# Attention with an ELU feed-forward on one core: another order of the first stage, and six weight tiles kept in PSUM

## The chip, the core and the metric

The kernel runs on one core of a Trainium2 chip. A core has TensorE (PE in the profile, with PEld for its weight loads), VectorE (DVE), ScalarE (ACT), GpSimd (POOL) and SyncE (SP), which here only issues transfers. Each engine works through its own instructions strictly in order and waits for the others by semaphores. PE writes to PSUM, which has eight banks; the other tiles lie in SBUF. The metric is the time of one execution on the device in microseconds; 608.86 before the change (median of three runs, 608.73 to 609.06).

## The reference

```python
scores_l = scale * q @ k^T, where |i - j| < 16, else -1e9          # local window, head size 64
scores_s = scale * q @ max over 32 keys of k + log(32)             # 24 block summaries
a = exp(scores - max);  a = a / (sum(a) + 1e-9)
x = a @ concat(v, mean over 32 of v)                               # 4 batches x 768 tokens x 512
h = x @ w_in                                                       # 512 -> 2048
g = where(h > 0, h, exp(min(h, 0)) - 1)
out = g @ w_out                                                    # 2048 -> 512
```

All is float32. The kernel multiplies in the format fp32r and splits each factor into a high half (rounded to fp32r) and a low half (what is left), and adds three products: high x high, low x high, high x low.

## The kernel before

The 3072 tokens go through the feed-forward in 6 chunks of 512, each in 16 steps f of 128 hidden columns. Step (c, f) makes `h` (12 products of 128x512, layer 1), takes `e = exp(h)` on ACT, forms the activation on DVE, splits it into `gh` and `gl`, and adds 12 products into four PSUM banks `o0` to `o3` (layer 2). The attention for the tokens of the next chunk runs between the steps, in groups of two pairs of heads: scores (`gsc`), maximum and mask on DVE (`glow`), exponentials on ACT (`ge`), reciprocal (`gz`), normalisation (`gn`), transposes (on PE, `gtr` with a copy `gpc`, or on DVE, `gb`), product with the values (`gval`), and the split of the result (`gxh`, `gxl`).

The first chunk is different. Its own attention has to run first (the words without a g: `sl`, `ss`, `low`, `exp`, `z`, `norm`, `tr`, `ptc`, `val`, `xh`, `xl`; `sums`, `spr` and `mv` make and spread the means of the values), and during its 16 steps the 32 weight tiles are loaded and split. Tile j (w1_f or w2_f) is loaded as 64-bit words (`w.j`), its lower bits are scaled on POOL or ACT (`X`, `Y`), its exponent is moved by ACT into a PSUM tile `sh` in bank a0 or a1 by j mod 2 (`M`), DVE joins the parts in two instructions into an SBUF tile `cv` with two buffers (`S`), the high half is cast (`H`, a second number 0 for ACT, 1 for POOL), and the low half is subtracted (`L`, 0 for POOL, 1 for DVE). The banks a0 and a1 also hold the scores and transposes of the attention groups. `first`, `L1h`, `L1l`, `L2a`, `L2b` and `L2c` are PE's products of chunk 0; `E`, `gap` and `larger` make the activation from h, `G` and `gl` split it.

The order of all this, on all five engines, is a list of words by hand, `FIRST`; each word stands for one such step (`name.arguments`), and each engine gets its instructions in the list's order. Short products into unused banks (`idle`, `warm`) fill PE's gaps before the first layer-1 product. Behind the list follows a loop over the remaining 80 steps, in which only PE and SP are in program order; a scheduler places the instructions of the others, and it may place the loop's first instructions between the last ones of the list.

Line numbers below are those of the kernel before: 152 and 155 the two joining instructions, 161 and 164 high and low half of a weight, 184 exponentials, 188 to 193 sum, reciprocal and normalisation, 202 transposes, 426 the first value products, 470 the first layer-1 products, 690 and 730 layers 1 and 2 of chunk 0, 679 and 740 the same in the loop, 695 the exponential of h, 699 and 710 the loop's minimum and sum.

Of the kernel before, what the change touches and what calls it, by code (L numbers as in the profile page):

```python
# [40 lines left out]
FIRST = """  # L41
    kq.2 mh.0 kq.3 sl.0 ve.3 ve.0 w.0 ve.1 mh.1 ss.0 idle.1.188 low.0.0 max.1 low.0.1 sl.1 idle.1.260 ss.1 ve.2
    max.2 exp.0.0 vo low.1.1 exp.0.1 exp.1.1 w.1 z.0 norm.0.1.0 norm.0.0.0 low.1.0 exp.1.0 w.5 max.3 sl.2 w.2 ss.2
    low.2.0 exp.2.0 z.1 norm.1.0.0 low.2.1 exp.2.1 sl.3 idle.1.232 ss.3 low.3.0 low.3.1 w.3 exp.3.1 z.2 tr.0.1.0
    tr.0.0.1 w.4 warm.2.288 sums.0 sums.1 warm.1.88 X.0 norm.1.1.0 ptc.0.0.0 norm.2.1.0 norm.2.0.0 exp.3.0 ptc.0.1.0
    w.7 sums.2 spr.3.0 spr.0.0 mv.0.0.0 tr.1.0.3 ptc.1.0.1 zh.3.1 sk.0 spr.2.0 spr.1.1 norm.3.1.0 mv.0.1.0 mv.0.2.0
    tr.2.1.1 w.9 warm.1.164 ptc.2.1.0 w.6 tr.2.0.0 ptc.2.0.1 mv.1.1.0 M.0 tr.1.1.2 ptc.1.1.1 mv.1.2.1 M.1 X.1 zh.3.0
    val.0.0 mv.0.3.0 mv.1.3.0 tr.3.1.0 ptc.3.1.1 norm.3.0.1 tr.3.0.0 mv.1.0.2 val.0.1 ptc.3.0.1 val.1.0 xh.0.0 S.0
    S.1 val.2.1 xl.0 val.1.1 xh.1.0 xl.1 H.0.1 val.2.0 xh.2.0 L.0.0 val.3.0 val.3.1 w.18 xh.3.0 xl.2 xl.3 first.0
    first.1 M.2 H.1.0 q.0 first.2 Y.5 first.3 X.2 S.2 X.3 L.1.0 X.4 L1h.1 M.3 S.3 E.0 gap.0 sk.2 vm.0 H.3.1 H.2.0  # L50
    sv.0 M.4 L1l.1 larger.0 G.0.0 L1h.2 L.3.0 L1l.2 sk.3 gl.0.0 L2a.0 w.10 w.16 M.5 E.1 L.2.1 Y.6 X.7 S.4 H.4.0
    L.4.0 S.5 M.6 ts.1 H.5.0 stt.1 L2c.0 L2b.0 G.1.0 L2a.1 L2c.1 L.5.0 M.7 gl.1.0 w.8 E.2 S.6 H.6.1 L.6.0 gap.2 S.7
    H.7.0 vs.0 larger.2 G.2.0 ks.3 sk.1 X.10 gsc.0 glow.0.0 L1h.3 glow.0.1 ge.0.0 w.13 L.7.1 X.9 ks.1 gl.2.0 gz.0.0
    X.8 M.8 gn.0.0.0 M.9 w.17 L1l.3 E.3 S.8 H.8.1 L.8.0 S.9 H.9.1 gap.3 larger.3 w.11 X.11 M.10 ge.0.1 S.10 L2b.1
    L2a.2 L2c.2 L1h.4 L1l.4 gz.0.1 gn.0.1.1 L2b.2 q.1 M.11 E.4 gtr.0.0 G.3.1 gl.3.0 gap.4 L.9.1 S.11 H.10.0
    gpc.0.0.1 L1h.5 w.12 X.13 M.12 w.19 X.12 w.20 gtr.0.1 larger.4 G.4.1 L.10.1 S.12 gpc.0.1.1 H.11.0 L.11.0 M.13
    S.13 vm.1 L1l.5 w.15 X.20 E.5 H.12.0 gap.5 H.13.0 L2a.3 X.17 larger.5 ks.2 L2c.3 vl gval.0 w.14 gsc.1 gl.4.1
    glow.1.0 sv.1 G.5.0 gxh.0 X.16 X.14 M.14 L1h.6 L1l.6 gxl.0 L1h.7 ge.1.0 E.6 glow.1.1 M.15 L.12.0 S.14 H.14.0
    L.13.0 X.15 L1l.7 X.18 ks.0 S.15 X.19 gz.1.0 gap.6 gn.1.0.0 L2b.3 gl.5.0 L2a.4 sv.2 L2b.4 L2c.4 pm.2 K.3 L.14.1
    w.25 M.16 S.16 gtr.1.0 larger.6 ge.1.1 gz.1.1 L2a.5 H.15.0 L.15.0 vs.2 M.17 S.17 H.16.0 gn.1.1.0 gpc.1.0.1 M.18  # L60
    w.23 pm.3 E.7 gap.7 L2b.5 L2c.5 X.25 G.6.1 H.17.0 gl.6.0 gtr.1.1 gpc.1.1.1 M.19 L.16.1 S.18 H.18.0 L1h.8 L1l.8
    larger.7 gval.1 G.7.0 sv.3 vs.3 L.17.0 S.19 E.8 gl.7.0 gxh.1 w.22 vs.1 gxl.1 q.2 K.2 gsc.2 H.19.0 gap.8 glow.2.0
    L2a.6 L2b.6 L2c.6 L.19.0 w.30 larger.8 ge.2.0 L1h.9 L1l.9 L.18.0 X.22 w.24 glow.2.1 M.20 gz.2.0 ge.2.1 mmul S.20
    gn.2.0.1 M.22 w.21 gz.2.1 mact X.23 E.9 L2a.7 L2b.7 L2c.7 X.24 L1h.10 L1l.10 gn.2.1.1 w.28 gb.2.0.4 M.21 X.30
    gap.9 X.21 larger.9 G.8.1 gl.8.0 H.20.0 L.20.0 S.21 gb.2.4.8 w.26 H.21.1 M.23 L.21.0 S.23 E.10 G.9.1 gl.9.0
    L1h.11 w.31 L1l.11 S.22 H.23.1 E.11 gb.2.8.12 gap.10 H.22.0 gap.11 larger.10 larger.11 M.25 q.3 w.29 L2a.8 L2b.8
    M.24 L2c.8 G.10.0 L.22.0 S.24 L2a.9 L2b.9 L2c.9 L.23.0 S.25 X.26 gl.10.1 L1h.12 mm G.11.1 X.29 L1l.12 E.12
    gap.12 H.25.0 w.27 X.27 gsc.3 gb.2.12.16 gval.2 K.4 gxh.2 gl.11.1 H.24.1 L2a.10 L2b.10 X.28 L2c.10 L.24.0
    glow.3.1 M.27 glow.3.0 L.25.0 gxl.2 S.27 H.27.1 L.27.0 M.26 S.26 H.26.1 ge.3.0 L1h.13 L1l.13 larger.12 M.29
    ge.3.1 gz.3.0 gn.3.0.0 S.29 E.13 gap.13 L1h.14 M.28 G.12.1 gz.3.1 L2a.11 gn.3.1.1 gl.12.0 L1l.14 E.14 L2b.11  # L70
    gap.14 X.31 L2c.11 L2a.12 L2b.12 L.26.1 gb.3.0.4 L2c.12 M.31 larger.13 H.29.0 L.29.0 larger.14 L1h.15 L1l.15
    S.28 H.28.1 gb.3.4.8 S.31 L.28.0 M.30 S.30 G.13.0 gl.13.0 gb.3.8.12 H.30.1 L.30.0 G.14.0 gl.14.0 E.15 gap.15
    H.31.0 L2a.13 L2b.13 L.31.0 gb.3.12.16 larger.15 L2c.13 L2a.14 q.4 gsc.4 glow.4.0 gval.3 gxh.3 gxl.3 L2b.14
    glow.4.1 ge.4.1 gz.4.1 ge.4.0 gn.4.1.1 G.15.1 gl.15.0 L2c.14 gz.4.0 gn.4.0.1
"""
# [846 lines left out]
```

## Time and profile before

| | |
|---|---|
| median of three runs | 608.86 us (608.73 to 609.06) |
| the profiled execution, and its span | 608.52 us, 606.8 us |
| PE busy in the span | 598.2 us, 99% |
| DVE, ACT, POOL busy | 64%, 43%, 40% |
| granted TensorE clock | 0.999 |
| moved from and to HBM | 50.8 MB read, 6.3 MB written |

The profile is of one execution; all times in it count from the span's start, and some 1.7 us of the execution's time lie outside the span. Products on PE are pipelined: one of 128x512 is shown with about 0.39 us, but the next starts 0.227 us later. So PE's pace is read from the starts, and its waits from the idle time in brackets.

### The profile page before, as it was taken

Reading aid. Unit: us, or ns where it says so; the run is one execution under the profiler, and the core shown is the slowest. Engines: PE = TensorE matmul, PEld = TensorE weight load, DVE = VectorE, ACT = ScalarE, POOL = GpSimd, SP = SyncE. Lnnn points to the kernel's source line nnn. Section 1 sums busy time; section 2 is a strip of 40 time slices with the busy share of each in tenths; the row PEclk is TensorE's granted clock in tenths of the full one; section 3 lists DMA queues with packets and bytes.
Section 4 is the critical chain, followed back from the end, with each engine's and each line's share of the span. In section 5 each row is a group of like instructions: output and inputs, shape, how many; then the busy total and the mean of one; then the engine's idle time right before and its main releaser. Section 6 shows DMA issues by size and latency. Waiting matters only on the chain.

```text
span 606.8 us, 11202 instructions
## 1 busy us (share of the span) xinstructions
PE 598.2 (99%) x4105; PEld 489.4 (81%) x4105; DVE 391.3 (64%) x1099; ACT 261.9 (43%) x754; POOL 245.7 (40%) x285
## 2 busy tenths in 40 slices
PE   9999999999999999999999999999999999999997
PEld 7787888878888888888888888888888888888885
DVE  7999989977667875656767676566575563222122
ACT  6987875654243343442433424425424332322222
POOL 5898998742333332332323323323133232222221
PEclk9999999999999999999999999999999999999999
DMA  9999783141005225220063132303111000100001
GB/s 313 376 362 310 219 292 85 32 136 47 23 27 146 78 72 177 71 66 0 28 174 109 53 94 80 102 2 107 60 38 42 2 1 0 70 0 1 0 1 69
DMA packets 63694, 58.62 MB, mean 97 GB/s; under 512 B 22664, under 2 KB 55176, under 8 KB 63640
## 3 DMA queue, kind: packets, MB, share of 16 engines
q1 hardware_dynamic: 60328, 52.02, 28.7%
q10 hardware_dynamic: 3312, 5.90, 2.6%
q8 instruction: 32, 0.52, 0.3%
q14 instruction: 22, 0.18, 0.1%
HBM read 50.82 MB, written 6.29 MB: 94 GB/s over the span
## 4 chain that ended last, share of the span: by engine, by line
PE 88%; DVE 5%; DMA 2%; issue 2%; ACT 1%; SPq 0%; DVEq 0%; ACTq 0%
PE h L679 36%; PE o L740 36%; PE o_ps L643 4%; PE o L730 4%; PE h L690 3%; PE s L586 3%; DMA vxh<-in_v_dram 2%; DVE sh L152 2%; DVE pt L624 1%; DMA kn<-in_kT_dram 1%; DVE cv L155 1%; PE t_ps L202 1%; PE o_ps L426 1%; DVE e L707 1%; PE h L470 0%
## 5 line engine op out<-in xcount | busy, mean ns | idle before, releaser
L720 POOL TENSOR_TENSOR gl<-e,gh 128x512 fp32r<-128x512 f32 x93 | 120.2, 1293 | 262.6 <-ACT gh L715 151.5
L679 PE MATMUL h<-xh,w 128*128 128x512 f32 x640 | 212.4, 393 | 0.0
L740 PE MATMUL o<-w,gh 128*128 128x512 f32 x648 | 163.0, 389 | 0.0
L740 PEld LDWEIGHTS o<-w,gh 128*128 128x128 f32 x648 | 121.7, 188 | 25.2
L679 PEld LDWEIGHTS h<-xh,w 128*128 128x128 f32 x640 | 120.2, 188 | 25.9
L695 ACT ACTIVATE e<-h 128x512 f32<-128x512 f32 x96 | 57.1, 595 | 182.9 <-PE h L679 169.4
L624 DVE STREAM_TRANSPOSE pt<-sm 32x256 f32<-32x256 f32 x288 | 125.6, 436 | 6.4 <-POOL sm L193 1.4
L699 DVE TENSOR_SCALAR e<-e 128x512 f32<-128x512 f32 x81 | 41.9, 517 | 133.7 <-ACT e L695 133.3
L679 PE MATMUL h<-xl,w 128*128 128x512 f32 x320 | 124.7, 390 | 0.0
L715 ACT CAST gh<-e 128x512 fp32r<-128x512 f32 x88 | 54.5, 621 | 103.9 <-DVE e L710 102.9
L740 PE MATMUL o<-w,gl 128*128 128x512 f32 x324 | 89.6, 389 | 0.0
L184 ACT ACTIVATE sm<-sm,mx 128x120 f32<-128x120 f32 x160 | 61.2, 385 | 24.0 <-DVE mx L176 24.0
L740 PEld LDWEIGHTS o<-w,gl 128*128 128x128 f32 x324 | 60.8, 188 | 12.6
L679 PEld LDWEIGHTS h<-xl,w 128*128 128x128 f32 x320 | 60.1, 188 | 11.9
L193 POOL TENSOR_TENSOR sm<-sm,z 128x480 f32<-128x480 f32 x34 | 35.9, 1075 | 64.0 <-DVE z L196 62.6
L710 DVE SCALAR_TENSOR_TENSOR e<-h,e 128x512 f32<-128x512 f32 x81 | 56.0, 692 | 2.8
L176 DVE CUSTOM_DVE_ANT_0 sm<-s,mask 128x120 f32<-128x120 f32 x160 | 34.2, 278 | 22.1 <-PE s L586 22.1
L690 PE MATMUL h<-xh,w 128*128 128x512 f32 x120 | 39.4, 395 | 0.0
L164 POOL TENSOR_TENSOR w<-cv,w 128x512 fp32r<-128x512 f32 x25 | 33.0, 1327 | 4.5 <-ACT w L161 3.5
L657 DVE TENSOR_TENSOR xl<-o_ps,xh 128x256 fp32r<-128x256 f32 x40 | 15.1, 419 | 26.3 <-ACT xh L650 26.3
L730 PE MATMUL o<-w,gh 128*128 128x512 f32 x120 | 31.8, 395 | 0.0
L184 ACT ACTIVATION_READ_ACCUMULATOR sm<-sm,mx 128x1 f32 x160 | 30.2, 189 | 0.0
(121 smaller groups left out, 555.5 us busy)
## 6 DMA issues: line engine op xcount, KB each, us to landing
...
```

The source lines that it names most:

```text
L184: nc.scalar.activation(out=sm[:, t, :], in_=sm[:, t, :], func=AF.Exp, bias=mx[:, t, :], scale=-1.0, accum_out=z[:, t, :])
L193: engine.tensor_tensor(out=sm, in0=sm, in1=z.broadcast_to([P, UW, KC]), op=ALU.mult)
L624: nc.vector.transpose(out=dst[k, :, q], in_=src[q, :, k])
L679: nc.tensor.matmul(h_ps, w[:, a, cols], bb[:, cc, :], start=(k == 0), stop=(k == 3 * NCC - 1))
L690: nc.tensor.matmul(h_ps, w[:, lo, cc * P:(cc + 1) * P], bb[:, cc, :], start=(lo, cc, i) == (0, 0, 0), stop=(lo, cc) == (1, NCC - 1))
L695: nc.scalar.activation(out=e, in_=h_ps, func=AF.Exp)
L699: nc.vector.tensor_scalar(out=e, in0=e, scalar1=1.0, scalar2=-1.0, op0=ALU.min, op1=ALU.add)
L710: top = nc.vector.scalar_tensor_tensor(out=e, in0=h_ps, scalar=0.0, in1=e, op0=ALU.max, op1=ALU.add)
L715: copy(out=gh, in_=e)
L720: engine.tensor_tensor(out=gl, in0=e, in1=gs[(c, f)][0].bitcast(F32), op=ALU.subtract)
L730: nc.tensor.matmul(o_acc[0][s], gs[(0, f)][a][:, s * P:(s + 1) * P], w[:, bb, :], start=(f, part) == (0, 0), stop=False)
L740: nc.tensor.matmul(o_acc[c][s], a[:, s * P:(s + 1) * P], w[:, bb, :], start=first and f == 0, stop=last and f == NF - 1)
```

## The change

The list is another one: the same steps (one short filling product more), in another order and in some places on another engine. The conversions 7, 9, 10, 14, 16 and 26 get a third number (`S.7.1`): their joined weight is written back into the PSUM tile `sh`, and cast and subtracted from there; their low halves are all on DVE. The constant 1e-9 is written once beside the places of the row sums of the first chunk's attention, and the addition before the reciprocal becomes a sum over the two numbers. One load of queries goes from ACT's queue to SP's, behind the second pair's keys.

```diff
-    kq.2 mh.0 kq.3 sl.0 ve.3 ve.0 w.0 ve.1 mh.1 ss.0 idle.1.188 low.0.0 max.1 low.0.1 sl.1 idle.1.260 ss.1 ve.2
+    kq.2 sl.0 mh.0 mh.1 max.1 kq.3 ss.0 low.0.1 low.0.0 exp.0.1 sl.1 w.0 ss.1 idle.1.164 exp.0.0 max.2 low.1.0
...
-    glow.4.1 ge.4.1 gz.4.1 ge.4.0 gn.4.1.1 G.15.1 gl.15.0 L2c.14 gz.4.0 gn.4.0.1
+    glow.4.0 ge.4.0 L.30.0 L2c.14 glow.4.1 G.15.1 gz.4.0 ge.4.1 gz.4.1 gl.15.0 gn.4.1.1 H.31.0 L.31.1 gn.4.0.0
...
-        def join(self):
+        def join(self, keep=False):
             bits = self.sh.bitcast(U32)
...
-            self.cv = ffn.tile([P, WC], F32, tag="cv", name="cv", bufs=2)
+            self.cv = self.sh if keep else ffn.tile([P, WC], F32, tag="cv", name="cv", bufs=2)
...
-    def reciprocals(z):
-        nc.vector.tensor_scalar(out=z, in0=z, scalar1=1e-9, scalar2=None, op0=ALU.add)
-        nc.vector.reciprocal(out=z, in_=z)
...
-        nc.scalar.dma_start(out=qn[0][:, 1], in_=qT[0, 1, :, 0:CH])
         nc.sync.dma_start(out=kn[1][:, E:E + S], in_=kT[0, 1])
+        nc.sync.dma_start(out=qn[0][:, 1], in_=qT[0, 1, :, 0:CH])
...
+        nc.vector.memset(small[:, 2 * NP:, :], 1e-9)
...
+        def inverted(p, heads):
+            z = small[:, 2 * p + heads.start:2 * p + heads.stop, UW:2 * UW]
+            nc.vector.tensor_reduce(out=z, in_=zs[p][:, heads], axis=AX.X, op=ALU.add)
+            nc.vector.reciprocal(out=z, in_=z)
...
-            "S": lambda j: conversion(j).join(), "H": ...
+            "S": lambda j, keep=0: conversion(j).join(keep), "H": ...
```

Three places show what the new list does to the instructions. The first is DVE, where the weights w1_5 (conversion 9, bank a1), w2_4 (10, a0) and w1_6 (11, a1) are joined, shortly before PE's first transposes of an attention group. Before:

```order
L152 SCALAR_TENSOR_TENSOR sh_857<-sh_857,raw_w2_4_686 128x512
L155 SCALAR_TENSOR_TENSOR cv_866<-raw_w2_4_686,sh_857 128x512
L812 RECIPROCAL z_859<-z_859 128x4
L193 TENSOR_TENSOR sm_793<-sm_793,z_859 128x4x120
L164 TENSOR_TENSOR w1_5_850<-cv_848,w1_5_850 128x512
L152 SCALAR_TENSOR_TENSOR sh_900<-sh_900,raw_w1_6_854 128x512
L155 SCALAR_TENSOR_TENSOR cv_916<-raw_w1_6_854,sh_900 128x512
```

And now, in the same place of DVE's order:

```order
L152 SCALAR_TENSOR_TENSOR sh_863<-sh_863,raw_w1_5_640 128x512
L155 SCALAR_TENSOR_TENSOR sh_863<-raw_w1_5_640,sh_863 128x512
L152 SCALAR_TENSOR_TENSOR sh_861<-sh_861,raw_w2_4_671 128x512
L155 SCALAR_TENSOR_TENSOR sh_861<-raw_w2_4_671,sh_861 128x512
L164 TENSOR_TENSOR w1_5_879<-sh_863,w1_5_879 128x512
L817 RECIPROCAL z_871<-z_871 128x4
L164 TENSOR_TENSOR w2_4_915<-sh_861,w2_4_915 128x512
L152 SCALAR_TENSOR_TENSOR sh_918<-sh_918,raw_w1_6_645 128x512
L155 SCALAR_TENSOR_TENSOR cv_921<-raw_w1_6_645,sh_918 128x512
```

The two tiles are now written to `sh` and subtracted from it, both on DVE, and the normalisation of the attention group (`sm`) is no longer on DVE.

The second place is ACT at the end of the list, where the loop begins; `h_1907` before and `h_1902` now are the loop's first layer-1 result, `w2_15` is the last weight tile of the list. Before:

```order
L695 ACTIVATE e_1797<-h_1751 128x512
L703 ACTIVATE e_1797<-e_1797 128x512
L161 CAST w2_15_1800<-cv_1774 128x512
L650 CAST xh_990<-o_ps_1850 128x256 x2
L184 ACTIVATE sm_1843,z_1880<-sm_1843,mx_1875 128x120 x4
L600 ACTIVATE z_1880<-z_1880,tiny_82 128x4
L184 ACTIVATE sm_1843,z_1887<-sm_1843,mx_1845 128x120 x4
L695 ACTIVATE e_1920<-h_1907 128x512
```

And now:

```order
L700 ACTIVATE e_1787<-h_1768 128x512
L655 CAST xh_977<-o_ps_1820 128x256 x2
L184 ACTIVATE sm_1859,z_1866<-sm_1859,mx_1861 128x120 x4
L605 ACTIVATE z_1866<-z_1866,tiny_82 128x4
L184 ACTIVATE sm_1859,z_1885<-sm_1859,mx_1877 128x120 x4
L700 ACTIVATE e_1915<-h_1902 128x512
L605 ACTIVATE z_1885<-z_1885,tiny_82 128x4
L161 CAST w2_15_1895<-cv_1791 128x512
```

The cast of w2_15 stood ahead of the last attention group's work, and stands now behind it and behind the exponential of the loop's first result.

The third place is DVE there. Before, the low half of w2_15 was not on DVE at all, and DVE's rows were:

```order
L812 RECIPROCAL z_1880<-z_1880 128x4
L193 TENSOR_TENSOR sm_1843<-sm_1843,z_1880 128x4x120
L699 TENSOR_SCALAR e_1920<-e_1920 128x512
L759 COPY ots_1928<-o1_679 128x512
L710 SCALAR_TENSOR_TENSOR e_1920<-h_1907,e_1920 128x512
L812 RECIPROCAL z_1887<-z_1887 128x4
L193 TENSOR_TENSOR sm_1843<-sm_1843,z_1887 128x4x120
```

And now:

```order
L817 RECIPROCAL z_1866<-z_1866 128x4
L704 TENSOR_SCALAR e_1915<-e_1915 128x512
L817 RECIPROCAL z_1885<-z_1885 128x4
L715 SCALAR_TENSOR_TENSOR e_1915<-h_1902,e_1915 128x512
L189 TENSOR_TENSOR sm_1859<-sm_1859,z_1885 128x4x120
L164 TENSOR_TENSOR w2_15_1895<-cv_1791,w2_15_1895 128x512
L764 COPY ots_1923<-o1_713 128x512
```

The low half of w2_15 stands behind two instructions of the loop's first step, which read `h_1902`.

## Rows read from the trace of the kernel before

**Rows 1.** Stretches: us, busy (instructions) of PE, PEld, DVE, ACT, POOL; clock, DMA, GB/s

```profile
25.00:50.00 25.00, 25.00 (x224) 20.70 (x220) 24.20 (x50) 20.19 (x48) 22.79 (x25) 1.00 1.05 368
...
250.00:300.00 50.00, 50.00 (x330) 41.16 (x329) 31.42 (x94) 17.63 (x56) 15.89 (x15) 1.00 0.10 28
```

**Rows 2.** Timeline of PE: start, duration, line, operation [idle before, what ended it]

```profile
26.79 0.50 PE L470 MATMUL h<-xh,w 128*128 128x512 f32 x1
...
49.30 1.07 PE L730 MATMUL o<-w,gl 128*128 128x512 f32 x4
50.89 0.62 PE L202 MATMUL t_ps<-ident,sm 128*120 128x128 f32 x4 [0.52 <-DVE z L812]
...
54.01 0.62 PE L202 MATMUL t_ps<-ident,sm 128*120 128x128 f32 x4 [0.65 <-DVE cv L155]
...
61.07 0.39 PE L690 MATMUL h<-xl,w 128*128 128x512 f32 x1 [0.53 <-issue]
...
125.70 1.03 PE L643 MATMUL o_ps<-pt,vw 120*64 120x64 f32 x28 [0.53 <-DVE pt L624]
```

**Rows 3.** Timeline of ACT, DVE and PE before the first product

```profile
19.25 0.19 ACT L184 ACTIVATION_READ_ACCUMULATOR sm_own<-sm_own,mean 128x1 f32 x1
...
21.65 0.91 DVE L193 TENSOR_TENSOR sm_own<-sm_own,mean 128x480 f32<-128x480 f32 x1
...
22.71 0.62 PE L202 MATMUL t_ps<-ident,sm_own 128*120 128x128 f32 x4 [0.62 <-ACT vxl L457]
23.38 0.68 PE L426 MATMUL o_ps<-pt_own,vxl 120*64 120x64 f32 x16
```

**Rows 4.** Timeline of PE at the hand-over to the loop

```profile
128.62 0.40 PE L679 MATMUL h<-xh,w 128*128 128x512 f32 x1
...
131.12 0.39 PE L679 MATMUL h<-xh,w 128*128 128x512 f32 x1
131.35 0.61 PE L740 MATMUL o<-w,gh 128*128 128x512 f32 x2
```

**Rows 5.** Groups of DVE's instructions from 25 to 130 us: busy, mean ns

```profile
L152 DVE SCALAR_TENSOR_TENSOR sh<-sh,raw_w 128x512 uint32<-128x512 uint32 x31 | 21.4, 692 | 1.1 <-POOL raw_w L140 0.6 <-ACT sh L148 0.3
...
L164 DVE TENSOR_TENSOR w<-cv,w 128x512 fp32r<-128x512 f32 x7 | 7.4, 1063 | 0.0
...
L193 DVE TENSOR_TENSOR sm<-sm,z 128x480 f32<-128x480 f32 x4 | 3.6, 890 | 0.1
...
L720 DVE TENSOR_TENSOR gl<-e,gh 128x512 fp32r<-128x512 f32 x3 | 2.1, 686 | 0.0
```

**Rows 6.** Lines 164 and 435 on DVE: shortest, median, longest ns

```profile
L164 DVE TENSOR_TENSOR w<-cv,w x7: 662/858/1776, 32.0 to 111.1; 128x512 fp32r<-128x512 f32 x7
...
L435 DVE TENSOR_TENSOR xl<-o_ps,xh x4: 680/680/683, 26.0 to 27.8; 128x512 fp32r<-128x512 f32 x4
```

**Rows 7.** Timeline of ACT around the hand-over

```profile
121.78 0.60 ACT L161 CAST w<-cv 128x512 fp32r<-128x512 f32 x1
...
131.83 0.58 ACT L695 ACTIVATE e<-h 128x512 f32<-128x512 f32 x1
...
132.78 0.30 ACT L600 ACTIVATE z<-z,tiny 128x4 f32<-128x4 f32 x1
```

**Rows 8.** Timeline of DVE at the hand-over

```profile
132.44 0.43 DVE L699 TENSOR_SCALAR e<-e 128x512 f32<-128x512 f32 x1 [1.12 <-ACT e L695]
...
133.52 0.68 DVE L710 SCALAR_TENSOR_TENSOR e<-h,e 128x512 f32<-128x512 f32 x1
134.12 0.17 DVE L812 RECIPROCAL z<-z 128x4 f32<-128x4 f32 x1
134.32 0.66 DVE L193 TENSOR_TENSOR sm<-sm,z 128x480 f32<-128x480 f32 x1
```

**Rows 9.** Stretches at the end

```profile
602.00:604.00 2.00, 0.74 (x4) 0.28 (x2) 0.69 (x1) 0.59 (x2) 0.00 (x0) 1.00 0.84 316
604.00:606.80 2.80, 0.00 (x0) 0.00 (x0) 0.00 (x0) 0.00 (x0) 0.00 (x0) 0.80 0.42 149
```

More of the change, by code (lines that the diff above doesn't have):

```diff
@@ L47 @@
[L47 to L66, printed above, removed]
@@ L72 @@
-    S.28 H.28.1 gb.3.4.8 S.31 L.28.0 M.30 S.30 G.13.0 gl.13.0 gb.3.8.12 H.30.1 L.30.0 G.14.0 gl.14.0 E.15 gap.15
-    H.31.0 L2a.13 L2b.13 L.31.0 gb.3.12.16 larger.15 L2c.13 L2a.14 q.4 gsc.4 glow.4.0 gval.3 gxh.3 gxl.3 L2b.14
-    glow.4.1 ge.4.1 gz.4.1 ge.4.0 gn.4.1.1 G.15.1 gl.15.0 L2c.14 gz.4.0 gn.4.0.1
+    kq.2 sl.0 mh.0 mh.1 max.1 kq.3 ss.0 low.0.1 low.0.0 exp.0.1 sl.1 w.0 ss.1 idle.1.164 exp.0.0 max.2 low.1.0
+    low.1.1 sl.2 ss.2 idle.1.168 max.3 exp.1.0 sl.3 ss.3 idle.1.180 z.0 low.2.0 norm.0.0.0 exp.1.1 exp.2.0 ve.0
@@ new lines @@
+    sums.0 idle.1.160 norm.0.1.0 tr.0.1.0 warm.1.192 low.2.1 z.1 norm.1.1.0 tr.1.1.2 norm.1.0.0 low.3.1 X.0 low.3.0
+    ptc.0.1.0 exp.2.1 z.2 exp.3.1 tr.0.0.1 ptc.0.0.0 ve.2 tr.1.0.3 ptc.1.0.0 ve.1 ve.3 sums.1 sums.2 warm.1.228
+    norm.2.1.0 tr.2.1.1 spr.3.1 mv.0.3.0 spr.0.1 exp.3.0 norm.2.0.1 zh.3.1 spr.2.0 spr.1.1 mv.0.0.0 mv.0.2.0 vo
+    norm.3.1.1 tr.2.0.0 warm.1.196 val.0.0 mv.1.3.0 w.1 w.2 w.5 ptc.2.0.1 tr.3.1.0 ptc.2.1.0 val.2.0 zh.3.0 M.0
+    ptc.1.1.1 norm.3.0.1 tr.3.0.0 S.0 mv.1.0.0 q.0 w.3 mv.0.1.0 sk.0 X.1 val.1.0 mv.1.1.1 w.6 mv.1.2.0 M.1 H.0.1
@@ new lines @@
+    L.0.0 ptc.3.0.1 ptc.3.1.1 X.2 w.7 val.0.1 xh.0.0 X.3 val.1.1 w.4 S.1 xl.0 xh.1.0 w.8 xl.1 val.2.1 xh.2.0 xl.2
+    vm.1 vl M.2 val.3.1 val.3.0 xh.3.0 xl.3 S.2 H.1.0 L.1.0 first.0 sv.0 H.2.1 first.1 first.2 Y.5 M.3 first.3 E.0
+    gap.0 S.3 H.3.0 w.9 larger.0 w.14 w.11 L.2.0 w.13 G.0.1 X.4 L.3.1 L1h.1 M.5 gl.0.0 S.5 X.7 w.10 L1l.1 E.1 gap.1
+    L1h.2 larger.1 M.4 H.5.0 G.1.0 L.5.0 sk.3 M.7 L1l.2 S.4 H.4.0 w.15 L2a.0 L2c.0 S.7.1 L2b.0 L1h.3 L1l.3 q.1 Y.6
+    M.6 L.4.0 S.6 H.7.0 L.7.1 gsc.0 E.2 gap.2 larger.2 L1h.4 L1l.4 gl.1.0 w.17 vm.0 H.6.0 L.6.1 w.18 ks.0 X.8 E.3
@@ new lines @@
+    glow.1.1 M.15 L1h.6 gz.1.0 L.14.1 X.19 M.16 L.13.0 S.15 sk.2 L1l.6 L2a.4 ge.1.1 L2b.4 S.16.1 vs.3 E.6 H.16.0
+    gz.1.1 L2c.4 L1h.7 L1l.7 H.15.0 gap.6 M.17 w.22 X.22 gl.5.0 E.7 w.20 L2a.5 L2b.5 gap.7 L.16.1 K.2 gn.1.0.0
+    gtr.1.0 larger.6 S.17 w.21 L1h.8 gn.1.1.0 gpc.1.0.1 larger.7 M.18 sv.2 gtr.1.1 gpc.1.1.1 L.15.0 M.19 G.6.1 w.28
+    L1l.8 vs.2 gl.6.0 q.2 E.8 gap.8 w.23 H.17.1 L2c.5 L2a.6 S.18 H.18.0 G.7.0 L.17.0 S.19 X.21 H.19.0 X.23 gval.1
+    gxh.1 vs.0 larger.8 gsc.2 glow.2.0 K.3 glow.2.1 L1h.9 q.3 L.18.0 gxl.1 ge.2.0 mmul mact X.20 M.21 L1l.9 ks.2
@@ L395, in exp_whole @@
             if p not in zs:
-                zs[p] = small[:, 2 * (NP + p):2 * (NP + p + 1), :].rearrange("p h (t o) -> p h t o", o=2)[:, :, :, 0:1]
+                sum_rows(p)
             nc.scalar.activation(out=sms[p][:, h], in_=sms[p][:, h], func=AF.Exp, scale=-1.0)
         def row_sums(p, h, by=0):
-            (nc.vector, nc.gpsimd)[by].tensor_reduce(out=zs[p][:, h].rearrange("p t o -> p (t o)"), in_=sms[p][:, h], axis=AX.X, op=ALU.add)
+            (nc.vector, nc.gpsimd)[by].tensor_reduce(out=zs[p][:, h, :, 0:1].rearrange("p t o -> p (t o)"), in_=sms[p][:, h], axis=AX.X, op=ALU.add)
         def recip(p):
-            reciprocals(zs[p])
+            inverted(p, slice(0, 2))
         def recip_head(p, h):
-            reciprocals(zs[p][:, h])
+            inverted(p, slice(h, h + 1))
         def mean_rows(i, first, end):
@@ L803, in attn_elu_ffn @@
             "X": lambda j: conversion(j).low_bits(), "Y": lambda j: conversion(j).low_bits_scaled(), "M": lambda j: conversion(j).exponent(),
-            "S": lambda j: conversion(j).join(), "H": lambda j, by=0: conversion(j).high((nc.scalar.copy, nc.gpsimd.tensor_copy, nc.vector.tensor_copy)[by]),
+            "S": lambda j, keep=0: conversion(j).join(keep), "H": lambda j, by=0: conversion(j).high((nc.scalar.copy, nc.gpsimd.tensor_copy, nc.vector.tensor_copy)[by]),
             "L": lambda j, by=0: conversion(j).rest((nc.gpsimd, nc.vector)[by]),
```

32 lines of the change are left out of this document (20 added, 12 removed).

## The prediction

> **What bounds the kernel now.** I read the page's busy shares first, then the stretches, then the order of TensorE's (PE's) own work, and last what each wait of PE was for. PE is busy for 99% of the span, and the other engines for 40 to 64% (the table of the profile). The stretches say where that average hides something: from 25 us on VectorE (DVE) is busy for 24.2 of 25 us, so there two engines are near their bound at once; from 250 on DVE has room (31.4 of 50) and PE has none [rows 1]. A product of 128x512 starts every 0.227 us (131.12 to 131.35 in [rows 4]). Time can thus come from three places only: the start of the first product of layer 1 at 26.79, PE's waits up to the end of the ordered list, and the hand-over to the loop at 131.35. In the loop the order of every engine is the same in both programs from its second step on.
>
> The waits are few. PE's rows with idle time in brackets give 0.52, 0.65, 0.53 and 0.53 us [rows 2]. The first ends with DVE's reciprocals, the second with DVE's second shift of a weight tile (the bank a1 that the transposes want still holds it), the third with nothing that the trace shows, the fourth with DVE's block transposes. By the spacing of starts they are a little longer: the four products at 49.30 would let the next one start at 50.21, it starts at 50.89, and a change of shape costs 0.1 anyway, so 0.58; in the same way the second is 0.71 and the fourth 0.60. With 0.2 to 0.3 of smaller delays I count 2.1 us that DVE causes, and 0.6 that has no known cause.
>
> **Part 1, up to the first product.** ScalarE's exponentials run in one row until 19.25. Behind them stand one normalisation on DVE (21.65, 0.91 us), the transposes at 22.71, and seven groups of value products on PE, 23.38 to 26.79, 0.49 us each [rows 2, 3]. After the change DVE takes the maxima of the second pair before the first scores, and two short copies of the means go to ScalarE ahead of the last four exponentials; so I let the exponentials end some 0.8 later (an estimate). DVE then has three normalisations, not one (0.9 each, 1.8 more), and one large copy less. The addition of 1e-9 ahead of each reciprocal goes, a reduction over as few numbers takes its place: a tiny instruction for another, which I cost at nothing, since DVE is then waiting for the exponentials anyway. The last normalisation ends near 22.5 again and the transposes start at 22.6, where they started at 22.71. Six value groups follow instead of seven, 6 x 0.49 = 2.9, so the first product stands near 26.3: -0.5 us. The moved load of queries goes behind the second pair's keys on SyncE's queue; the keys land some 0.6 earlier, these queries as much later, and the second scores on PE start near 6.5 instead of 7.05: nothing. Bounds: -1.3, if DVE's chain is not late and only PE's groups count; +0.5, if POOL's seven copies of the means hold a value group.
>
> **Part 2, the ordered list to its end.** DVE's load changes by kinds: four more subtractions of a weight, three fewer of an activation, four fewer normalisations: 4 x 1.06 - 3 x 0.69 - 4 x 0.89 = -1.4 us [rows 5]. POOL gets those and gives up four weight subtractions and four casts; by 1.3 and 0.6 each that is even. What decides is the order. Up to the shift that frees a1 for the second transposes, DVE now does ten conversions (twice 0.69 each [rows 5]), five weight subtractions, four maxima of activations, two reductions and the scores of one group: about 23.5 us behind the last attention subtraction. That ended at 28.5 (four of 0.68, the last at 27.8 [rows 6]) and ends now near 28.1, so a1 is free near 52.3 with 0.7 of DVE's own waits. PE, with 26.2 us of work and 0.6 of shape changes behind 26.3, asks for it at 53.1: 0.8 to spare, where before it asked at 53.3 and got it at 54.01. The group's second normalisation, whose reciprocal ended the first wait, is on POOL now with several microseconds to spare, and DVE reaches the block transposes of the fourth group some 3 us sooner. I take -2.0 us for the part. Bounds: -2.9, if the unexplained wait goes too; 0, if the kept tiles only move the waits.
>
> The kept tiles cut both ways: the shifted weight stays in a0 or a1 through a cast on ScalarE and a subtraction on DVE, some 1.3 us longer each, but that subtraction reads PSUM. Its price lies between two rows: the four subtractions that read PSUM took 0.680 to 0.683 each, the seven weight subtractions from SBUF 0.66 to 1.78 [rows 6]. I take 0.7 for the six kept ones, as the operands are those of the first row. The Trainium skill (GPSIMD Engine Reference, Specifications) says that POOL shares its SBUF interfaces with VectorE and that a DVE instruction with two SBUF inputs contends with it. The rows agree: only the form with two SBUF inputs spreads. By that rule three kept tiles ahead of the second transposes save 3 x 0.38 = 1.1 us of DVE time against the mean of 1.06; without it the 0.8 to spare would be gone.
>
> **Part 3, the hand-over.** The list now ends with the last weight tile, w2_15: its high half is cast on ScalarE behind both heads' exponentials of group 4, and its low half is subtracted on DVE as the very last. The order of the built program shows more: the loop's first exponential (of h_1902, the loop's first product group) stands on ScalarE ahead of that cast, and on DVE the loop's minimum, a reciprocal, the loop's sum, a normalisation all stand ahead of that subtraction. PE needs w2_15 straight behind the group that fills h_1902. Before, the tile was done long ahead, and PE went on at 131.35 without a gap [rows 4]. Now, with t for the start of that group (12 products, 2.73 us to the next start; its last result at t + 2.89): the exponential starts near t + 3.0, as ScalarE's exponentials for group 4 end about then (the scores are read 2.1 us before t, from the first score to this exponential ScalarE and DVE need about 5 us of work), and takes 0.58; the minimum 0.43, the reciprocal 0.17, the sum 0.68, the normalisation 0.66 [rows 7, 8]; the subtraction 0.66 at least. With 0.03 between them it ends near t + 6.4. The cast, behind exponential and bias (0.58, 0.30 and 0.60), is done at t + 4.5, which lets one product through. PE wanted the low half at t + 2.96: a wait of 3.4 us, in which nothing else can run on PE, since everything on it stands behind in order. Bounds: 3.1, if neighbours on DVE overlap by 0.08, as the sum and the reciprocal do in [rows 8] (133.52 + 0.68 against 134.12), and 4.5, if the subtraction takes the longest of its rows, 1.78.
>
> **Sum.** -0.5 - 2.0 + 3.4 = +0.9 us against the profiled execution's 608.52, so 609.4; the median of the runs is 0.34 higher, so 609.8, 0.15% above 608.86. Less than 0.2% (1.2 us) can't be told from no change here.
>
> **Rivals.**
> B. *The kept tiles move the waits.* Where the next conversions wait for a bank one subtraction longer, ScalarE, which issues them in order, stands, and with it casts and exponentials. For it: DVE at 97% from 25 us on [rows 1] and only 0.8 us to spare at the second transposes. Against: fewer DVE microseconds in all. Decides where DVE is over 0.8 us later than I walked it. Then part 2 gives 0, part 1 -0.2, the hand-over 3.4: +3.2, 612.1, slower.
> C. *The last tile is not waited for so long*, because it is converted before the loop's own work: -2.5, 606.4, faster. For it: the list itself has no loop work in it, and DVE has room there. Against: the built order, in which h_1902 must be full before DVE reaches the tile. Decides if the wait at the hand-over is under 1.2 us.
> D. *The clock falls in the hand-over.* PE would stand for about 1.6 us, run one product, and stand for 1.9. In the trace the granted clock is full in every stretch of work; PE's last work ends at 602.74 (busy for 0.74 of the stretch from 602), and the clock is 1.00 up to 604 and 0.80 on average in the next 2.8 us [rows 9], so it falls near 605.7, after some 2.9 us without work: longer than either wait. If it fell to the lower level (1.2 GHz) for as long as the wait, each product of 0.227 would take twice that, +1.7: 611.5. The Trainium skill (TensorE: Matmul & The Clock Gate, Why this matters for your kernels) warns that an idle gap between bursts returns the array to its lower level; by that rule D would be the forecast only if the two waits count as one.
>
> **Chances.** The forecast 0.62 (its own range 608.6 to 611.0), B 0.18, C 0.10, D 0.08, anything else 0.02. Range: 607.7 to 612.1; it takes in the bounds of the three parts but for the ends together, and leaves out C. Some 0.4 of the forecast lies above 610.08, as do B and D; nearly all of C lies below 607.64: faster 0.10, same 0.46, slower 0.44.
>
> **What would show it.** In the profile after: a PE wait of about 3 us or more just before the first products with w2_15, ended by a DVE subtraction that writes w, near 127 to 134 us; the first layer-1 product at 25.5 to 27.3; no wait for a shift, reciprocal or block transpose over 0.3 us before that; kept subtractions near 0.7. Wrong is the forecast if the hand-over's wait is under 2.5 us, or if PE's waits between 30 and 125 us add up to more than 1.5.

## The result, and the profile after

The changed kernel is slower by 1.1%: 615.87 us median against 608.73 of the kernel before on the same chip, 13 runs each, ratio 1.011 (95% interval 1.0086 to 1.0134). The forecast was 609.8 with a range to 612.1, so it was wrong. More telling than the median is the spread: before, the runs lie between 608.36 and 609.33; after, between 610.81 and 618.74. The profiled execution is the fastest of these, 610.81 us with a span of 609.1. It can only explain part of the loss, and the experiments have to find the rest.

PE in the start, after: start, duration, line, operation [idle before, what ended it].

```profile
5.87 0.97 PE L377 MATMUL s<-ks,qn 64*64 64x24 f32 x32
7.47 0.89 PE L377 MATMUL s<-kn,qn 64*64 64x96 f32 x32 [0.62 <-DMA qn<-in_qT_dram]
...
21.50 0.69 PE L431 MATMUL o_ps<-pt_own,vxh 120*64 120x64 f32 x16 [0.39 <-POOL vxh L462]
...
24.17 0.69 PE L431 MATMUL o_ps<-pt_own,vxh 120*64 120x64 f32 x16 [0.20 <-POOL vxh L462]
...
27.34 0.50 PE L475 MATMUL h<-xh,w 128*128 128x512 f32 x1
```

The second pair's scores start at 7.47 and wait for the load of queries that the change moved to SP's queue. Before, a filling product stood ahead of them, and they started without a wait:

```profile
6.53 0.59 PE L280 MATMUL idle<-kw 128*128 128x188 f32 x2
7.05 0.89 PE L380 MATMUL s<-kn,qn 64*64 64x96 f32 x32
```

Later the values wait twice for POOL's copies of the means, and the chain of work that leads to the first product runs through these copies (POOL, 19.80 to 24.12). The first product stands at 27.34, where [rows 2] have 26.79: 0.55 later.

PE's waits from 27 to 135 us, after: for what, how long, how often, the longest.

```profile
PE o L745 <- ACT w L161: 1.7, 1, 1.7
PE o L745 <- DVE w L164: 1.1, 1, 1.1
PE h L695 <- DVE e L712: 0.7, 1, 0.7
```

The waits of [rows 2] for a reciprocal, a shift and a block transpose are gone; one of 0.7 for an activation is new. The loop's first product group starts at 126.04, before at 128.62 [rows 4]: the stage from the first product to there takes 98.70 us instead of 101.83, 3.13 less. The waits are half of that: 2.23 us in the brackets of [rows 2] against 0.7 now. PE has the same 741 products there in both traces, so the other 1.6 lie in delays too short to be listed as waits. The two other lines are the hand-over. PE there, after:

```profile
128.54 0.39 PE L684 MATMUL h<-xh,w 128*128 128x512 f32 x1
130.60 0.47 PE L745 MATMUL o<-w,gh 128*128 128x512 f32 x1 [1.67 <-ACT w L161]
132.16 0.50 PE L745 MATMUL o<-w,gh 128*128 128x512 f32 x1 [1.09 <-DVE w L164]
132.50 0.40 PE L745 MATMUL o<-w,gl 128*128 128x512 f32 x1
132.73 0.84 PE L745 MATMUL o<-w,gh 128*128 128x512 f32 x2
133.37 0.63 PE L745 MATMUL o<-w,gl 128*128 128x512 f32 x1
133.80 1.05 PE L745 MATMUL o<-w,gh 128*128 128x512 f32 x2
...
136.36 0.41 PE L684 MATMUL h<-xh,w 128*128 128x512 f32 x1
```

In [rows 4] a product follows the last of the group after 0.23 us. Now it is 2.06 (128.54 to 130.60), and the next one after 1.56: less 0.23 each, 3.17 us of standing. Behind the waits the next rows show something else: the product at 133.37 is followed by the next one after 0.43 us instead of 0.227. That is the granted clock (stretches, us: busy and instructions of PE, PEld, DVE, ACT, POOL; clock; DMA share; GB/s):

```profile
133.00:136.00 3.00, 3.00 (x9) 2.33 (x8) 1.92 (x5) 1.10 (x2) 0.25 (x1) 0.50 0.35 136
136.50:140.00 3.50, 3.50 (x17) 2.87 (x16) 1.66 (x4) 1.19 (x2) 0.00 (x0) 1.00 0.42 153
```

By the clock's records of this trace it is at 1.2 GHz from 132.97 to 136.38, 3.41 us, in which half the work is done: 1.7 us lost. DVE and ACT there, after, which [rows 7, 8] answer to:

```profile
129.79 0.43 DVE L704 TENSOR_SCALAR e<-e 128x512 f32<-128x512 f32 x1 [1.82 <-ACT e L700]
130.13 0.17 DVE L817 RECIPROCAL z<-z 128x4 f32<-128x4 f32 x1
130.25 0.69 DVE L715 SCALAR_TENSOR_TENSOR e<-h,e 128x512 f32<-128x512 f32 x1
130.86 0.65 DVE L189 TENSOR_TENSOR sm<-sm,z 128x480 f32<-128x480 f32 x1
131.43 0.69 DVE L164 TENSOR_TENSOR w<-cv,w 128x512 fp32r<-128x512 f32 x1
```

```profile
129.18 0.57 ACT L700 ACTIVATE e<-h 128x512 f32<-128x512 f32 x1
129.66 0.29 ACT L605 ACTIVATE z<-z,tiny 128x4 f32<-128x4 f32 x1
129.85 0.61 ACT L161 CAST w<-cv 128x512 fp32r<-128x512 f32 x1
```

The last weight tile stands behind the loop's minimum, sum and a normalisation, and its cast behind the loop's exponential, as the built order had it.

The profiled execution adds up: +0.55 (first product) - 3.13 (stage) + 3.17 (hand-over) + 1.7 (clock) = +2.29, and 610.81 - 608.52 = 2.29. What is missing is why the typical run is 5 us longer still.

### The profile page after: what moved, and what is told of

The parts are those of the page before. It is cut to its first block, busy times and chain, and to the rows that moved or that the text cites. A ratio compares the mean times of both kernels' runs of the same rounds, so it can differ in the third digit from the quotient of the medians.

```text
span 609.1 us, 11193 instructions
## 1 busy us (share of the span) xinstructions
PE 598.9 (98%) x4105; PEld 490.9 (81%) x4105; DVE 387.5 (64%) x1097; ACT 264.9 (43%) x760; POOL 241.6 (40%) x282
## 4 chain that ended last, share of the span: by engine, by line
PE 92%; ACT 2%; DMA 2%; DVE 1%; POOL 1%; issue 0%; SPq 0%; POOLq 0%; DVEq 0%
PE o L745 36%; PE h L684 36%; PE h L695 6%; PE o L735 5%; PE o_ps L648 3%; PE s L591 3%; ACT sm_own L184 1%; DMA n<-in_vT_dram 1%; DMA raw_w<-in_w_in_dram 1%; PE idle L276 1%; PE o_ps L431 1%; ACT sm L184 0%; PE h L475 0%; PE t_ps L198 0%; POOL vxh L462 0%
## 5 line engine op out<-in xcount | busy, mean ns | idle before, releaser
L725 POOL TENSOR_TENSOR gl<-e,gh 128x512 fp32r<-128x512 f32 x96 | 123.8, 1290 | 265.2 <-ACT gh L720 155.4
L189 POOL TENSOR_TENSOR sm<-sm,z 128x480 f32<-128x480 f32 x38 | 40.1, 1072 | 67.8 <-DVE z L192 63.1
L662 DVE TENSOR_TENSOR xl<-o_ps,xh 128x256 fp32r<-128x256 f32 x40 | 15.1, 420 | 26.3 <-ACT xh L655 26.2
L164 POOL TENSOR_TENSOR w<-cv,w 128x512 fp32r<-128x512 f32 x21 | 27.3, 1302 | 2.1 <-ACT w L161 1.2
```

Source lines behind the costliest of these rows:

```text
L725: engine.tensor_tensor(out=gl, in0=e, in1=gs[(c, f)][0].bitcast(F32), op=ALU.subtract)
```

## Experiments

Ratios are to the kernel before, run on the same chip beside each group of runs (its medians there 608.79 to 608.97).

| run | what it is | runs in us | median | ratio (95%) |
|---|---|---|---|---|
| e1 | the change again | 615.41 | | |
| e2 | last tile early | 605.7 to 607.3 (5), 610.6 to 612.5 (7) | 610.68 | 1.0009 (0.9985, 1.0034) |
| e3 | PE filled in the hand-over | 609.6 to 609.8 (4), 613.8 to 615.8 (5) | 613.75 | 1.0059 (1.0034, 1.0084) |
| e4 | before, last tile late | 612.3 to 614.9 (4) | 613.98 | 1.0089 (1.0075, 1.0104) |
| e5 | e2, query load back on ACT | 605.2 to 606.6 (9), 607.4, 608.0, 612.0 | 605.84 | 0.9961 (0.9943, 0.9978) |
| e6 | e2, PE filled at 6 us | 605.7 to 606.5 (7), 607.6, 608.4, 609.1 | 606.32 | 0.9964 (0.9952, 0.9976) |
| e7 | the change, query load back | 608.3 to 614.2 (10) | 610.47 | 1.0028 (1.0008, 1.0048) |
| e8 | before, with the gap at 6 us | 608.6 to 609.5 (6), 615.9 to 616.6 (4) | 609.52 | 1.0049 (1.0016, 1.0083) |
| e9 | e5 with a short filling at 6 us | 605.1 to 606.0 (7), 607.3 to 609.5 (5) | 605.94 | 0.9968 (0.9953, 0.9982) |
| e10 | e9, four kept tiles undone | 606.3 to 607.3 (10), 609.1, 610.7 | 606.80 | 0.9976 (0.9964, 0.9988) |
| e11 | e9 with a longer filling | 605.2 to 606.0 (4), 606.7, 607.5 | 605.77 | 0.9954 (0.9942, 0.9966) |

Two theories stood at first: theory 1, that the hand-over alone loses the clock, for a time that varies; and theory 2, that the spread comes from the start.

**e1: the change again.** No edit.

> The changed kernel once more, for another profile of it. Its 13 runs lay between 610.81 and 618.74 us, and the profiled one was the fastest. Theory 1 (the two waits for the last weight tile at the hand-over make the clock fall, and it stays down for a varying time): a time of 614 to 618, the granted clock full up to about 133 us, and then 1.2 GHz for a stretch of 10 to 25 us, where the first profile has 3.4. Theory 2 (the clock is late or falls in the start, where it first rose at 6.7 us instead of 4.9): the stretch at the lower level lies ahead of 27 us, and the one behind the hand-over stays at 3.4.

It took 615.41 us. PE at the start:

```profile
4.54 1.56 PE L377 MATMUL s<-kn,qn 64*64 64x96 f32 x32
5.88 1.01 PE L377 MATMUL s<-ks,qn 64*64 64x24 f32 x32
7.62 1.56 PE L377 MATMUL s<-kn,qn 64*64 64x96 f32 x32 [0.74 <-DMA qn<-in_qT_dram]
...
34.56 0.50 PE L475 MATMUL h<-xh,w 128*128 128x512 f32 x1
```

The same 32 score products that took 0.89 us in the first profile take 1.56, and the first product stands at 34.56 instead of 27.34. The clock's records of this trace begin only at 24.4 us, so its mean clock reads 1.00; the pace shows the lower level before. The scores at 4.54 take 1.56 in the first profile too; there the clock rises at 6.7, ahead of the gap, and here it had not risen when the gap of 0.74 came. So in this execution it did not fall, it stayed down. From 34.56 the stage takes 97.72 us (the engines that feed PE have run ahead meanwhile, so its 0.7 of waiting goes too), and the two waits at the hand-over are the same 1.67 and 1.10, this time with no fall of the clock. 7.22 later in the start, 0.98 won in the stage, 1.7 not lost at the hand-over: +4.54 against the first profile, and 615.41 - 610.81 = 4.60. So in this run the loss lies in the start, and theory 1 doesn't explain it.

**e2: the last tile early.** The changed kernel with two words of the list moved:

```diff
-    ... L2a.13 L2b.13 L2c.13 L2a.14 stt.15 gl.14.0 ...
-    ... gn.4.1.1 H.31.0 L.31.1 gn.4.0.0
+    ... L2a.13 L2b.13 L2c.13 L2a.14 stt.15 H.31.0 L.31.1 gl.14.0 ...
+    ... gn.4.1.1 gn.4.0.0
```

> The two words for the last weight tile's halves stand right behind the addition of the list's last activation, ahead of the last attention group; all else is as in the changed kernel. Theory 1: no wait over 0.4 us at the hand-over, the clock full from about 7 us to the end, hardly any spread (under 1 us), and a time of about 606.2: the hand-over was reached 2.6 us ahead of before, and 608.7 - 2.6 is 606.1. Theory 2: the 3.2 us of waits go, but the clock still falls in most runs: 607 to 615, with a spread of several us.

The hand-over has no wait left, and five runs lie at 605.7 to 607.3, as theory 1 had it for all. But seven lie at 610.6 to 612.5, as theory 2 had it. The medians of the two groups, 606.36 and 611.05, are 4.7 us apart. The mean clock of the seven is 0.986 to 0.989, but for one that reads 1.000 as e1's did: this is the price of a low clock, and e1 and e3 place it in the start. The profiled run is of the lower group, and PE waited in it as well: its scores start so:

```profile
7.36 0.89 PE L377 MATMUL s<-kn,qn 64*64 64x96 f32 x32 [1.41 <-DMA qn<-in_qT_dram]
```

**e3: PE filled in the hand-over.** The changed kernel with work for PE between the loop's first h and the first products with the last tile:

```diff
+            if n == NF:
+                spare = psum.tile([P, CH], F32, tag="a0", name="spare")
+                for _ in range(11):
+                    nc.tensor.matmul(spare[:, 0:P], ident, ident, start=True, stop=True)
```

> The changed kernel with eleven short products of 128x128 into an unused bank on PE between the group that fills the loop's first h and the first products with the last weight tile, so that PE has about 2.5 us of work inside its wait. Theory 1: the waiting stays (3.2 us, now partly filled), the clock doesn't fall, and the time is 609 to 610 with a spread under 1 us: 606.1 + 3.2. Theory 2: 611 to 618 as before, since the waits are not what lowers the clock.

Again two groups. In the lower one (609.6 to 609.8) no run is spread by the hand-over, and its median lies 3.4 us above that of e2's lower group, the 3.2 us of standing and 0.2. The profiled run is of the upper group, and here the clock's records reach into the start. PE, and then the stretch:

```profile
7.70 0.89 PE L377 MATMUL s<-kn,qn 64*64 64x96 f32 x32 [1.37 <-DMA qn<-in_qT_dram]
...
33.21 0.50 PE L475 MATMUL h<-xh,w 128*128 128x512 f32 x1
```

```profile
9.00:22.60 13.60, 13.45 (x132) 10.90 (x131) 7.88 (x56) 9.36 (x49) 4.51 (x5) 0.50 1.06 358
23.00:27.00 4.00, 4.00 (x61) 3.27 (x59) 3.17 (x8) 1.65 (x8) 2.31 (x3) 1.00 1.07 367
```

The clock is granted in full at the scores, then halved soon behind PE's wait of 1.37, and stays there for 13.6 us in which PE is busy nearly all the time. The same stretch of e2's profile, with a wait of 1.41 ahead of it, is at full clock and holds 220 of PE's records instead of 132:

```profile
9.00:22.60 13.60, 13.07 (x220) 10.76 (x220) 12.62 (x68) 12.42 (x62) 8.77 (x11) 1.00 1.05 355
```

So the fall comes behind a wait, and the length of the wait alone does not decide it. The first rise differs too: by the clock's records it comes at 5.6 us here, at 4.9 in the profile before and at 6.7 in the one after, and e2's first scores run at the full pace from 4.54 on (0.90 for the same 32 products).

**e4: before, with the last tile late.** The kernel before with one edit:

```diff
-    H.31.0 L2a.13 L2b.13 L.31.0 gb.3.12.16 ... gz.4.0 gn.4.0.1
+    L2a.13 L2b.13 gb.3.12.16 ... gz.4.0 gn.4.0.1 H.31.0 L.31.1
```

> The kernel before with one edit: the two words for the last weight tile's halves stand at the end of its list, the low half on DVE, as in the changed kernel. Theory 1: two waits of together 3 to 3.5 us at the hand-over, the clock falls behind them, and the time is 612 to 621 with a spread of several us. Theory 2: the same waits, a full clock, and about 612 with hardly any spread.

The shortest run, 612.27, is 3.4 above before; the others are 1.6 to 2.6 longer still. The profile is that of the shortest:

```profile
131.56 0.39 PE L679 MATMUL h<-xh,w 128*128 128x512 f32 x1
133.68 0.47 PE L740 MATMUL o<-w,gh 128*128 128x512 f32 x1 [1.73 <-ACT w L161]
135.24 0.50 PE L740 MATMUL o<-w,gh 128*128 128x512 f32 x1 [1.10 <-DVE w L164]
135.58 0.39 PE L740 MATMUL o<-w,gl 128*128 128x512 f32 x1
135.81 0.62 PE L740 MATMUL o<-w,gh 128*128 128x512 f32 x2
```

Standing of 1.89 + 1.33 = 3.22 us, and products at full pace behind it. So the hand-over is worth 3.2 us by itself, and up to 2.6 more where the clock falls; that this is what the three longer runs lost is what their mean clocks (0.997, 0.993, 0.996) suggest, and no profile of one was taken.

That left the start. Theory A: the moved load of queries lands late, PE stands at 6 us, and that loses the clock. Rival B: another part of the new start does it.

**e5: the load back.** e2 with

```diff
+        nc.scalar.dma_start(out=qn[0][:, 1], in_=qT[0, 1, :, 0:CH])
         nc.sync.dma_start(out=kn[1][:, E:E + S], in_=kT[0, 1])
-        nc.sync.dma_start(out=qn[0][:, 1], in_=qT[0, 1, :, 0:CH])
```

> As the version with the early last tile, but the one load of queries is issued by ACT again, ahead of the second pair's keys, as in the kernel before. Theory A (the moved load lands at 7.2 to 7.6 us instead of 5.5, PE stands for 0.6 to 1.4 us ahead of the second pair's scores, and that keeps the clock down or lets it fall for about 15 us in two runs of three): PE's wait there shrinks to what the keys need (landing near 6.5, so 0 to 0.6), the clock is full from 7.3 us at the latest to the end in nearly every run, and the time is 605.0 to 606.2 with a spread under 1.5 us. Rival B (the new start loses the clock elsewhere, by its fewer filling products or by PE's waits at 14.5, 21.5 and 24.2 us): two groups of times as without this edit, near 606 and near 611.

Nine of twelve runs are at 605.2 to 606.6, where five of twelve were below 607.3. Three are not, and the profile is of one of these (608.01). PE still stood, now for the keys, and the clock was low in a stretch that begins only 7 us later:

```profile
7.43 0.89 PE L377 MATMUL s<-kn,qn 64*64 64x96 f32 x32 [0.81 <-DMA kn<-in_kT_dram]
```

```profile
4.00:14.00 10.00, 8.70 (x212) 6.93 (x211) 7.75 (x44) 5.50 (x29) 2.89 (x20) 1.00 1.04 344
14.40:21.10 6.70, 6.55 (x34) 4.96 (x38) 4.25 (x30) 4.80 (x26) 4.79 (x6) 0.50 1.06 382
```

**e6: the gap filled, the load still late.** e2 with one word more, `idle.1.440`, behind `ss.0`:

```diff
-    kq.2 sl.0 mh.0 mh.1 max.1 kq.3 ss.0 low.0.1 ...
+    kq.2 sl.0 mh.0 mh.1 max.1 kq.3 ss.0 idle.1.440 low.0.1 ...
```

> As the version with the early last tile, the load of queries still on SP, with one filling product of 128x440 (about 1.4 us at the full clock) between the first pair's block scores and the second pair's scores. Theory A, in which the gap in PE's work lowers the clock: the queries still land at 7.2 to 7.6, PE is busy until then, the clock stays up, and the time is 605.7 to 607.5 in all runs. If the late queries cost by their lateness and not by the clock, or under rival B: again two groups, near 606 and near 611.

Seven of ten runs are at 605.7 to 606.5 and none is above 609.2; the group at 610.6 to 612.5 is gone, though the queries come as late as before. Three runs lie above the 607.5 that theory A allowed, the longest by 1.6 us. In the profile the filling takes 1.00 us, not the 1.4 expected, and PE still waits a little:

```profile
7.91 0.89 PE L377 MATMUL s<-kn,qn 64*64 64x96 f32 x32 [0.37 <-DMA qn<-in_qT_dram]
```

The scores start later than in any other trace, and the time is near the lowest. So it is the gap in PE's work and not the lateness of the scores that costs.

**e7: the change with only the load back.** The edit of e5 in the changed kernel.

> The changed kernel with only the load of queries put back on ACT; the last weight tile stays late. Theory A: the start keeps its clock, so only the hand-over is left: 605.7 + 3.2 = 608.9 where the clock stays up there, and 1 to 3 us more where it falls behind the two waits: 608.5 to 612, none at 614 to 618. Rival B: 609 to 618 as the changed kernel.

608.3 to 614.2, six of ten at or below 610.9 and none at 615 to 618. Three of the runs (612.38, 613.52, 614.17) are above the 612 that theory A allowed. With e5's outliers in view that may be a rest of the same loss in the start and a fall at the hand-over together; no profile of such a run shows it. In the profiled one (608.33) the scores start at 6.97 without a bracket, and the first product stands at 26.99:

```profile
6.97 0.98 PE L377 MATMUL s<-kn,qn 64*64 64x96 f32 x32
```

**e8: the gap made in the kernel before.** Load moved as the change does, and the filling product ahead of the second scores left out:

```diff
-    ... mh.1 ss.0 idle.1.188 low.0.0 max.1 low.0.1 sl.1 ...
+    ... mh.1 ss.0 low.0.0 max.1 low.0.1 sl.1 ...
```

> The kernel before with two edits at the start: the load of queries moved to SP behind the second pair's keys, as the change does, and the filling product of 128x188 ahead of the second pair's scores left out. Theory A: PE stands for 0.6 to 1.4 us from about 6 us on, the clock is down until 20 to 25 us in many of the runs, and the times are in two groups, near 609 and near 613 to 614. Rival B: 608.7 to 609.5 in all runs, since the rest of the start is that of the kernel before.

Two groups, six runs at 608.6 to 609.5 and four at 615.9 to 616.6: with no other part of the new list the gap costs 7 us in four runs of ten, more than the 4 to 5 that I expected. The mean clock of the four is 0.986. They ran on the same chip as e5 and e6, so it isn't another chip that took e2's upper group away there. Rival B falls as the main cause. The profiled run is one of the six, and here too PE waited, 1.09 us:

```profile
7.69 0.89 PE L380 MATMUL s<-kn,qn 64*64 64x96 f32 x32 [1.09 <-DMA qn<-in_qT_dram]
```

**e9: all three edits.** e5 with `idle.1.188` behind `ss.0`, as the kernel before has it.

> The early last tile and the load of queries on ACT, and the filling product of 128x188 between the first pair's block scores and the second pair's scores, where the kernel before has it. Theory A: what is left of PE's gap there is under 0.3 us, so the runs with a lost clock (608.0 and 612.0 without the filling) go: 605.2 to 606.5 in all runs, faster than both kernels by 0.5% and 1.6%. If the outliers come from PE's later waits in the start (the values, 20 to 25 us): one or two of twelve runs still at 607 to 612.

A miss in part: seven of twelve as expected, five at 607.3 to 609.5. No run is at 610 or above, but this is no better than e5. PE's waits up to 135 us in the profiled run, one of the seven:

```profile
PE h L695 <- DVE e L712: 0.6, 1, 0.6
PE t_ps L198 <- DVE sm_own L189: 0.4, 1, 0.4
PE s L377 <- DMA kn<-in_kT_dram: 0.3, 1, 0.3
PE t_ps L198 <- ACT vsx L455: 0.2, 1, 0.2
```

**e10: four kept tiles undone.** e9 with `S.7`, `S.9`, `S.14` and `S.16` for `S.7.1` and so on; 10 and 26 stay kept.

> The same, with four of the six kept tiles (7, 9, 14 and 16) joined into an SBUF tile as in the kernel before; 10 and 26 stay kept. If the kept tiles are what took the stage's waits away: PE waits of 0.5 to 1.5 us between 45 and 75 us return and the time is 606.0 to 607.5. If the order of the list did it and the kept tiles only spare DVE time that nobody waits for: no wait over 0.3 us more, 605.2 to 606.3.

The lower group (ten runs, median 606.70) is 0.9 above e9's (seven runs, 605.82), and its shortest run, 606.28, is above the longest of e9's seven, 606.04. Over all runs the two ratios' intervals overlap. The first product and the loop's first, of e10 and then of e9:

```profile
27.24 0.50 PE L475 MATMUL h<-xh,w 128*128 128x512 f32 x1
...
126.84 0.39 PE L684 MATMUL h<-xh,w 128*128 128x512 f32 x1
```

```profile
27.68 0.50 PE L475 MATMUL h<-xh,w 128*128 128x512 f32 x1
...
126.19 0.39 PE L684 MATMUL h<-xh,w 128*128 128x512 f32 x1
```

The stage takes 99.60 and 98.51 us: by this pair four kept tiles are worth 1.1 of the 3.3 that e9 gains over [rows 2, 4], by the lower groups 0.9. A pair of traces can't carry that alone, since with all six tiles kept the stage took from 97.76 (e11) to 99.67 us (e2, with a wait of 1.06 for POOL). What the rest comes from, the order or the other small edits, was not taken apart. The large waits that were expected between 45 and 75 us don't return: PE's wait for an activation is 0.68 instead of 0.60, and one of 0.21 comes at 71.53.

**e11: the filling widened.** e9 with `idle.1.400`.

> As the version with all three edits, with the filling product widened from 128x188 to 128x400, so that PE has work until about 7.2 us at the full clock and the second pair's keys (landing 6.5 to 7.3) leave it no gap. If what is left of the gap at 6 us is what still loses the clock in 5 of 12 runs (607.3 to 609.5): all runs at 605.3 to 606.6. If these come from elsewhere in the new start: again 3 to 5 of 12 runs at 607 to 610.

PE had no wait at the second scores in the profiled run. Four of six runs at 605.2 to 606.0, one at 606.66 and one at 607.46: nothing at 608 or above, but with six runs this doesn't settle what the last outliers come from. It has the lowest median, 0.46% below the kernel before, but its interval overlaps those of e5, e6 and e9.

## Why the prediction was wrong

**The step that failed is one of part 1:** "the second scores on PE start near 6.5 instead of 7.05: nothing", on the moved load of queries. I let the queries land as much later as the keys landed earlier. They came far later: the scores that need them start at 7.36 to 7.70 in five traces with the moved load, and PE, which has no filling product there any more, stands for 0.62 to 1.41 us. What this gap does to the clock was not in the working at all. It costs 4.7 us in seven runs of twelve (e2), and is shown from both sides: it goes where the load goes back or the gap is filled (e5, e6), and comes to the kernel before with the gap (e8). The forecast counted waits one by one in time, and the gap could have been read in the order: a product of 128x188 stood ahead of these scores, and the new list has none. Neither of the two signs that were to show the forecast wrong came (the waits at the hand-over add up to 2.76 by the brackets, PE's waits before it to 0.7): both were set for waits, and none for the clock in the start.

**The rest of part 1 failed too, at a smaller price.** It was put at -0.5, and the first product came at +0.55, just outside the bound of +0.5. The reason given for that bound, that POOL's copies of the means hold a value group, is what the trace shows (waits of 0.39 and 0.20). The moved load is not the whole of it: with the load back the first product stands at 26.99, 27.24 and 27.68 (e7, e10, e9), and in none of these near the 26.3 of the forecast.

**Rival D had the mechanism and was priced too low.** It was given 0.08, because the only fall in the trace of before came after 2.9 us without work [rows 9], longer than either wait. Here the clock fell behind waits of 1.67 and 1.09 with one product between, and in the start behind one of 1.37 (e3); behind one of 0.74 it stayed down (e1). At the hand-over the size was right, 1.7 us in the profile; the place that matters was another. The Trainium skill (TensorE: Matmul & The Clock Gate, Why this matters for your kernels) had the warning that an idle gap brings the lower level. The gaps that it warns of are longer than the 1.37 us of e3 and the 1.67 and 1.09 of the changed kernel, and there the measurement decides. One trace with a fall after 2.9 us gave no bound from below.

**Right were part 3 and, in the main, the mechanism of part 2.** The hand-over's standing was put at 3.4 us (3.1 to 4.5) and is 3.17, with the last tile behind the loop's own work as read from the built order; e4 gives 3.22 for it in the kernel before, and e2 takes it away. The prediction's rival C falls. Part 2 was put at -2.0 (-2.9 to 0) and is -3.13, beyond its bound: the three waits for DVE went as walked, the one that had no known cause went too, and the new one of 0.7 was not foreseen. These five make -1.5 by the brackets. The other -1.6 is in short delays, which the working put at 0.2 to 0.3: that term was mis-sized. The prediction's rival B falls, since the stage gained and did not stand still; the kept tiles help, by 0.9 us for four of them if the lower groups of e9 and e10 are compared. Their subtractions, taken at 0.7, are these (shortest, median, longest ns, after):

```profile
L164 DVE TENSOR_TENSOR w<-sh,w x6: 660/684/692, 40.4 to 108.9; 128x512 fp32r<-128x512 f32 x6
L164 DVE TENSOR_TENSOR w<-cv,w x5: 684/980/1315, 32.7 to 131.4; 128x512 fp32r<-128x512 f32 x5
```

Six tiles that read PSUM spread by 0.03 us, five from SBUF by 0.63, as [rows 6] had it.

The terms without the clock (+0.55 - 3.13 + 3.17) give +0.6, against +0.9 forecast. That this comes so close is luck: part 1 was 1.05 too low and part 2 1.1 too high, and the two cancel. With 4.7 in the start and 1.7 at the hand-over, which a run may or may not have, that is 608.73 + 7.0 = 615.7 for one with both; the median is 615.87. Six of the 13 runs are 1 to 3 us longer than that. A start like e1's, which cost 6.2 net, would make 617.1 with the 1.7 of the hand-over; what the two longest (618.63, 618.74) lost beyond is not shown.

**Open:** why about the same wait is followed by a low clock in some executions and not in others; and what the runs that still lose 1 to 6 us (three of twelve in e5, three of ten in e6, five of twelve in e9) lose it to. A profile shows one of them (e5, low from 14.4 to 21.1 us, long after the wait of 0.81), and no run takes it away for sure.
